# Attention, mixer and FFN on one core: transposed scores, row sums as a value column, the mixer inside the attention loop, a token-major FFN with a table gelu

## The chip, the cores and the metric

The kernel runs on one core of one Trainium2 chip. The metric is the device time of one execution in microseconds; the kernel before took 1292.27 us, the median of three runs. A NeuronCore has five engines with an instruction queue each: TensorE (PE, matmuls into PSUM), VectorE (DVE), ScalarE (ACT), GpSimd (POOL) and SyncE (SP), which here issues transfers. They run side by side and wait for one another through semaphores; within a queue the order is fixed when the program is built.

## What is computed

```python
xn = layernorm(A_x)                                    # [2048, 576]
# attention: 32 query heads, 16 key/value heads, the last 512 keys of the cache
q = (xn @ wq).reshape(1, 2048, 32, 128).transpose(0, 2, 1, 3)
k = repeat(k_cache[:, :, 1536:, :], 2, axis=1); v = the same of v_cache
scores = einsum("bhqd,bhkd->bhqk", q, k) * 128 ** -0.5
s = softmax(scores) @ v, heads joined, @ wo            # [2048, 576]
# branch B, from the same xn
h  = gelu_tanh(layernorm(xn) @ w1)                     # four groups of 144 columns
hs = concat(h[g] shifted by +1, -1, +2, -2 tokens) @ w2
x1 = xn + hs
h2 = gelu_tanh(layernorm(x1) @ w3) @ w4                # w3 [576, 4608]
out = A_x + s * silu(x1 + h2)
```

All inputs are bf16, with normal entries times 0.05 (weights also divided by the root of their rows).

## The kernel before

Tokens go in four blocks of 512 (`QB`), each of four tiles of 128 rows; the model width 576 is four chunks of 128 and one of 64, so a projection is five accumulating matmuls of 512 columns. Program order is written by hand in Python loops; each engine takes its instructions in that order as far as its queue is concerned, and pools of SBUF and PSUM buffers add the waits.

Part A (0 to 782 us of the trace) runs over blocks and, within one, over 32 heads; one head of one block is called a unit below. `stage1(h)` makes the projection (L257), copies it to SBUF on ACT (`qT_hb`, L261), and for each tile of 128 tokens makes scores `[token, key]` (L270), the negated row maximum on DVE (L272), the exponential on ACT with that maximum as bias and the row sum as accumulator (L274), and on DVE the reciprocal (L279) and the scaling of the probabilities (L281). `stage2(h)`, two heads later, turns the probabilities round: for each of four key chunks four 128x128 transposes on TensorE (L292), a copy to SBUF (three on DVE, L298, one on ACT, L296), and one product with the values (L299, 512 columns), and then a copy of the head's output on ACT (L301). The output projection `wo` of the block before (L339, 512 and 64 columns for each head and token tile) is cut into pieces of eight heads, one piece a step; that of the last block stands alone at the end. The four normalized blocks go to DRAM (`xn_dram`) and the output projection's result to `s_dram`.

Part B loads xn again, loads and rearranges w1, w2 and w3, and runs the mixer block by block (782 to 899 us): a second layernorm with a square root on ACT (L115), transposes (L440), the up product with a five-step gelu on DVE and ACT (L446 to L456), the shifted down product of eight chunks a tile (four big, four with 16 rows; L487, L494), the addition (L500), a third layernorm and its transposes (L510, L512). Then the FFN (899 to 1287 us): for each block 36 steps of an up product with 4608/36 = 128 outputs (L580), the gelu chain copy (L556), square (L558), polynomial (L560), product (L563), Sigmoid on ACT (L565), product (L566), and two steps later a down product with weights w4 as the stationary side (L590), so that the result comes out with features on partitions; it is copied (L594), turned back by transposes (L599), and joined on DVE and ACT with x1, silu, s and A_x (L602 to L618).

Of the kernel before, what the change touches and what calls it, by code (L numbers as in the profile page):

```python
# [27 lines left out]
def kernel(  # L28
# [14 lines left out]
    nc = tc.nc  # L43

    Bb, S, D = A_x.shape
    assert Bb == 1
    _, Hkv, Sk, Dh = A_k_cache.shape
    assert Dh == P
    HqDh = A_wq.shape[1]
    Hq = HqDh // Dh  # L50
# [3 lines left out]
    assert W % P == 0  # L54
    KCH = W // P
    F = B_w3.shape[1]
    assert F % P == 0
# [3 lines left out]
    assert S % QB == 0  # L61
# [3 lines left out]

    DCH = []
    st = 0
    while st < D:
        w = min(P, D - st)
        DCH.append((st, w))  # L70
        st += w
    NDC = len(DCH)
    DLAST_W = DCH[-1][1]
    OSPLIT = []
    st = 0
    while st < D:
        w = min(512, D - st)
        OSPLIT.append((st, w))
        st += w
# [9 lines left out]
    const_pool = ctx.enter_context(tc.tile_pool(name="const_pool", bufs=1))  # L89
    ident = const_pool.tile([P, P], BF16, name="ident")  # L90
    make_identity(nc, ident)

    xn_dram_pool = ctx.enter_context(tc.tile_pool(name="xn_dram_pool", bufs=1, space=bass.MemoryType.DRAM))
    xn_dram = xn_dram_pool.tile([S, D], BF16, name="xn_dram")
    s_dram_pool = ctx.enter_context(tc.tile_pool(name="s_dram_pool", bufs=1, space=bass.MemoryType.DRAM))
    s_dram = s_dram_pool.tile([S, D], BF16, name="s_dram")

    eps_t = const_pool.tile([P, 1], FP32, name="eps_t")
    nc.vector.memset(eps_t[:], LN_EPS)

    def layernorm_rows(dsts, srcs, pool):
        n = len(srcs)
        ngrp = 1
        while D // ngrp > nc.vector.BN_STATS_FMAX or D % ngrp != 0:
            ngrp += 1
        fsz = D // ngrp
        mv = pool.tile([P, n, nc.vector.BN_AGGR_DIM], FP32, name="ln_mv")
        for i, src_ap in enumerate(srcs):
            stats = pool.tile([P, ngrp, nc.vector.BN_STATS_DIM], FP32, name="ln_stats")
            srcr = src_ap.rearrange("p (n f) -> p n f", f=fsz)  # L110
            for j in range(ngrp):
                nc.vector.bn_stats(out=stats[:, j, :], in_=srcr[:, j, :])
            nc.vector.bn_aggr(out=mv[:, i, :], in_=stats[:])
        rstd = pool.tile([P, n], FP32, name="ln_rstd")
        nc.scalar.activation(out=rstd[:, :], in_=mv[:, :, 1], func=ACT.Sqrt, bias=eps_t[:], scale=1.0)  # L115
        nc.vector.reciprocal(out=rstd[:, :], in_=rstd[:, :])
        for i, (dst_ap, src_ap) in enumerate(zip(dsts, srcs)):
            nc.vector.tensor_scalar(out=dst_ap, in0=src_ap, scalar1=mv[:, i, 0:1], scalar2=rstd[:, i:i + 1],
                                    op0=ALU.subtract, op1=ALU.mult)

    def _unused_transpose_tokens_to_T(src_tm, dstT, ps_pool, name):
        for b in range(NB):
            for kc, (cst, cw) in enumerate(DCH):
                ps = ps_pool.tile([P, QB], BF16, name=name, tag="tp")
                for tt in range(TB):
                    t = b * TB + tt
                    nc.tensor.transpose(out=ps[:cw, tt * P:(tt + 1) * P], in_=src_tm[:, t, cst:cst + cw],
                                        identity=ident[:, :])
                nc.scalar.activation(out=dstT[:cw, kc, b * QB:(b + 1) * QB], in_=ps[:cw, :], func=ACT.Copy)

    with ExitStack() as actx:
        a_big = actx.enter_context(tc.tile_pool(name="a_big", bufs=1))
        xnT = a_big.tile([P, NDC, S], BF16, name="xnT")
        if DLAST_W < P:
            nc.vector.memset(xnT[DLAST_W:, NDC - 1, :], 0.0)
        kT = a_big.tile([P, Hkv, W], BF16, name="kT")
        v_sb = a_big.tile([P, Hkv, KCH, Dh], BF16, name="v_sb")
        wo_sb = a_big.tile([P, Hq, D], BF16, name="wo_sb")
        oT_blks = [a_big.tile([P, Hq, QB], BF16, name=f"oT_blk{i}") for i in range(min(NB, 2))]
        xraw = actx.enter_context(tc.tile_pool(name="xraw", bufs=min(NB, 3)))  # L140
        xload = actx.enter_context(tc.tile_pool(name="xload", bufs=1))
        pro_small = actx.enter_context(tc.tile_pool(name="pro_small", bufs=4))
        wo_out = actx.enter_context(tc.tile_pool(name="wo_out", bufs=2))
        a_ld = actx.enter_context(tc.tile_pool(name="a_ld", bufs=2))
        wq_pool = actx.enter_context(tc.tile_pool(name="wq_pool", bufs=2))
        qt_pool = actx.enter_context(tc.tile_pool(name="qt_pool", bufs=3))
        p_pool = actx.enter_context(tc.tile_pool(name="p_pool", bufs=3))
        pt_pool = actx.enter_context(tc.tile_pool(name="pt_pool", bufs=4))
        small = actx.enter_context(tc.tile_pool(name="a_small", bufs=8))
        ps_tp = actx.enter_context(tc.tile_pool(name="ps_tp", bufs=2, space=bass.MemoryType.PSUM))  # L150
        ps_q = actx.enter_context(tc.tile_pool(name="ps_q", bufs=1, space=bass.MemoryType.PSUM))
        ps_sc = actx.enter_context(tc.tile_pool(name="ps_sc", bufs=4, space=bass.MemoryType.PSUM))
        ps_o = actx.enter_context(tc.tile_pool(name="ps_o", bufs=1, space=bass.MemoryType.PSUM))
# [495 lines left out]
```

## Time and profile before

| | us |
|---|---|
| median of three runs | 1292.27 (1289.19 to 1296.06) |
| span of the profiled execution | 1287.0 |
| attention, to the last output product | 0 to 782 |
| mixer, with the reload ahead of it | 782 to 899 |
| FFN | 899 to 1287 |
| busy over the span: TensorE, VectorE, ScalarE | 1073.4, 988.5, 829.3 |

The rows used are listed below. Busy time is the sum of what each record covers. Records of TensorE's matmuls overlap with those of their neighbours (a 512-column matmul is shown with about 380 ns), so what an engine can do in a stretch is read from the distance between starts. A row of the timeline joins several instructions of one line: its time is from the first start to the last end. "Idle before" is time in which the engine waited ahead of that group, with what ended the wait.

### The profile page before, as it was taken

To read this page: it belongs to the slowest core of one execution; us is meant where nothing else is said; L and a number is where in the kernel's file an instruction comes from. 1 tells how busy PE (TensorE), PEld (TensorE's weight loads), DVE (VectorE), ACT (ScalarE), POOL (GpSimd) and SP (SyncE) were. 2 spreads that over 40 slices of the span, in tenths; PEclk is the share of its full clock that TensorE was granted. 3 is DMA by queue.
4 is the path that set the end of the run, shared out by engine and by line. 5 is a ranking of instruction groups with operands and counts; after the bars stand their busy time and mean duration, and the time that the engine had idled before them with its cause. 6 is when DMAs were issued, how large, how long until landed. Compare 5 with 4: busy or idle time off the path is not lost.

```text
span 1287.0 us, 19414 instructions
## 1 busy us (share of the span) xinstructions
PE 1073.4 (83%) x6788; PEld 534.2 (42%) x6916; DVE 988.5 (77%) x2703; ACT 829.3 (64%) x1876; POOL 27.8 (2%) x41
## 2 busy tenths in 40 slices
PE   4777788998879997789997893696998898998995
PEld 2344444554445554445444451343433333433432
DVE  7999988788997879988889932796666766666665
ACT  5787887778887778877778830564545444544544
POOL 4100000000000000000000001001000000000000
PEclk9999999999999999999999997799999999998998
DMA  9402101001010010101101006213300101001001
GB/s 301 124 28 69 50 24 38 29 25 42 20 37 24 24 43 24 38 19 35 36 24 38 1 10 230 76 38 102 106 1 15 41 1 32 25 1 40 16 1 37
DMA packets 49954, 59.94 MB, mean 47 GB/s; under 512 B 11712, under 2 KB 46208, under 8 KB 49280
## 3 DMA queue, kind: packets, MB, share of 16 engines
q1 hardware_dynamic: 41968, 35.87, 9.2%
q0 software_dynamic: 3760, 13.97, 3.5%
q10 hardware_dynamic: 4128, 8.85, 2.1%
q8 instruction: 54, 0.88, 0.3%
q14 instruction: 44, 0.36, 0.1%
HBM read 51.60 MB, written 7.08 MB: 46 GB/s over the span
## 4 chain that ended last, share of the span: by engine, by line
PE 32%; ACT 30%; DVE 25%; issue 9%; DMA 3%; ACTq 0%; POOL 0%; SPq 0%; DVEq 0%
ACT p_blk L274 16%; PE pswo L339 7%; PE pso L299 6%; PE sc L270 5%; ACT g_hb L556 5%; DVE g_sq L558 4%; DVE g_arg L563 4%; DVE negmax L272 4%; DVE pT L298 3%; PE ptp L292 3%; DVE p_blk L281 3%; DVE g_u L560 3%; PE psq L257 3%; ACT oT_blk L301 2%; PE ps_h L590 2%
## 5 line engine op out<-in xcount | busy, mean ns | idle before, releaser
L274 ACT ACTIVATE p_blk<-sc,negmax 128x512 bf16<-128x512 f32 x512 | 346.6, 688 | 86.3 <-DVE negmax L272 85.0
L272 DVE TENSOR_REDUCE negmax<-sc 128x1 f32<-128x512 f32 x512 | 324.9, 684 | 28.6 <-PE sc L270 26.6
L299 PE MATMUL pso<-pT,v_sb 128*128 128x512 bf16 x512 | 187.4, 380 | 81.4 <-DVE pT L298 69.3
L565 ACT ACTIVATE g_sg<-g_arg 128x512 bf16<-128x512 bf16 x144 | 90.8, 631 | 179.7 <-DVE g_arg L563 179.5
L590 PE MATMUL ps_h<-h3g,w_sb 128*128 128x512 bf16 x718 | 177.3, 378 | 28.8 <-DVE h3g L566 15.4
L292 PEld LDWEIGHTS <-p_blk 128*128 128x128 bf16 x2048 | 145.5, 98 | 128.6 <-issue 59.2
L292 PE MATMUL ptp<-ident,p_blk 128*128 128x128 bf16 x2048 | 178.6, 219 | 7.3 <-DVE pT L298 3.0
L580 PE MATMUL ph<-x1nT,w_sb 128*128 128x512 bf16 x692 | 179.3, 386 | 4.6 <-ACT g_hb L556 2.2
L270 PE MATMUL sc<-kT,qT_hb 128*128 128x512 bf16 x496 | 154.6, 381 | 18.4 <-ACT qT_hb L261 16.0
L298 DVE COPY pT<-ptp 128x512 bf16<-128x512 bf16 x384 | 154.6, 413 | 17.7 <-PE ptp L292 16.5
L257 PE MATMUL psq<-xnT,wq_slab 128*128 128x512 bf16 x606 | 163.0, 381 | 2.1 <-ACT qT_hb L261 0.6
L339 PE MATMUL pswo<-wo_sb,oT_blk 128*128 128x512 bf16 (+1 forms) x985 | 157.6, 282 | 2.1 <-ACT p_blk L274 0.7
L281 DVE TENSOR_SCALAR p_blk<-p_blk,rinv 128x512 bf16<-128x512 bf16 x512 | 156.4, 348 | 2.0
L566 DVE TENSOR_TENSOR h3g<-g_hb,g_sg 128x512 bf16<-128x512 bf16 x144 | 61.3, 426 | 97.4 <-ACT g_sg L565 96.7
L590 PEld LDWEIGHTS <-w_sb 128*128 128x128 bf16 x720 | 69.6, 97 | 133.1 <-issue 61.6
L580 PEld LDWEIGHTS <-w_sb 128*128 128x128 bf16 x720 | 71.2, 99 | 90.7 <-issue 9.2
L274 ACT ACTIVATION_READ_ACCUMULATOR p_blk<-sc,negmax 128x1 f32 x512 | 105.0, 205 | 0.0
L339 PEld LDWEIGHTS <-oT_blk 128*128 128x128 bf16 x1024 | 73.8, 98 | 67.3 <-issue 11.3
L301 ACT ACTIVATE oT_blk<-pso 128x512 bf16<-128x512 f32 x128 | 76.3, 596 | 35.7 <-PE pso L299 35.7
L296 ACT ACTIVATE pT<-ptp 128x512 bf16<-128x512 bf16 x128 | 76.9, 601 | 23.9 <-PE ptp L292 23.9
L299 PEld LDWEIGHTS <-v_sb 128*128 128x128 bf16 x512 | 49.8, 98 | 95.6 <-DVE pT L298 57.1
L556 ACT ACTIVATE g_hb<-ph 128x512 bf16<-128x512 f32 x144 | 83.6, 581 | 7.5 <-PE ph L580 4.6
(84 smaller groups left out, 857.4 us busy)
## 6 DMA issues: line engine op xcount, KB each, us to landing
wq_slab<-in_A_wq_dram SPq DMA_DIRECT2D x30, 512.0 KB, 3.5
w_sb<-in_B_w_dram POOLq DMA_DIRECT2D x4, 1296.0 KB, 12.2
wo_sb<-in_A_wo_dram POOLq DMA_DIRECT2D x4, 1152.0 KB, 13.5
w_sb<-in_B_w_dram ACTq DMA_DIRECT2D x1, 4608.0 KB, 18.5
xn_dram<-xnb SPq DMA_DIRECT2D x4, 576.0 KB, 3.2
s_dram<-s_out SPq DMA_DIRECT2D x16, 144.0 KB, 1.8
xnb<-xn_dram SPq DMA_DIRECT2D x4, 576.0 KB, 4.7
xnt<-xn_dram ACTq DMA_DIRECT2D x16, 144.0 KB, 2.1
```

What stands on the lines that cost most here:

```text
L257: nc.tensor.matmul(psq[:, :], lhsT=wq_slab[:, kc, hh * Dh:(hh + 1) * Dh], rhs=xnT[:, kc, qb * QB:(qb + 1) * QB], start=(kc == 0), stop=(kc ...
L270: nc.tensor.matmul(sc[:, :W], lhsT=qT_hb[:, qc * P:(qc + 1) * P], rhs=kT[:, g, :], start=True, stop=True)
L272: nc.vector.tensor_reduce(out=negmax[:, qc:qc + 1], in_=sc[:, :W], axis=AX.X, op=ALU.max, negate=True)
L274: nc.scalar.activation(out=p_blk[:, qc, :], in_=sc[:, :W], func=ACT.Exp, bias=negmax[:, qc:qc + 1], scale=1.0, accum_out=rowsum[:, qc:qc + 1])
L281: nc.vector.tensor_scalar_mul(out=p_blk[:, qq, :], in0=p_blk[:, qq, :], scalar1=rinv[:, qq:qq + 1])
L292: nc.tensor.transpose(out=ptp[:, qc * P:(qc + 1) * P], in_=p_blk[:, qc, kc * P:(kc + 1) * P], identity=ident[:, :])
L298: nc.vector.tensor_copy(out=pT[:, :], in_=ptp[:, :])
L299: nc.tensor.matmul(pso[:, :], lhsT=v_sb[:, g, kc, :], rhs=pT[:, :], start=(kc == 0), stop=(kc == KCH - 1))
L339: nc.tensor.matmul(ps[:, :dw], lhsT=lhsT, rhs=wo_sb[:, h, dst:dst + dw], start=(h == 0), stop=(h == Hq - 1))
L556: nc.scalar.activation(out=hb[:, :], in_=ps_ap, func=ACT.Copy)
L580: nc.tensor.matmul(ph3[:, :], lhsT=w3_sb[:, kc, fc * P:(fc + 1) * P], rhs=x1nT[:, kc, b * QB:(b + 1) * QB], start=(kc == 0), stop=(kc == N ...
L590: nc.tensor.matmul(ph2s[dc][:, :], lhsT=w4_sb[:, fc2, dc * P:(dc + 1) * P], rhs=h3g[:, :], start=(fc2 == 0), stop=(fc2 == FC - 1))
```

## The change

Attention is one loop over 128 units with four stages. `stage_q(u+1)` is the projection and its copy. `stage_s(u)` makes the scores transposed: key chunk as the stationary side, `sc` is `[128 keys, 512 tokens]`, and one exponential with the score scale gives `pT`, with no maximum and no bias. `stage_v(u-1)` takes slices of `pT` as weights and the values with an added column of ones (`VW = Dh + 2`, 129 columns used) as the moving side, so that column 129 of the result is the row sum; DVE takes its reciprocal and multiplies. `stage_t(u-2)` transposes the head's output, with a DVE copy. A table `fill` puts the other work at fixed units: the output projection of the block before at units 2 to 6 of a block, the second layernorm, its transposes and the mixer's up product at 8 to 15, its down product at 16 to 20 (of the block before; of the last block also at 22 to 26), the next block's layernorm and transposes at 21 to 26. xn stays in SBUF, x1 goes to `x1_dram`. The layernorm takes its square root by three Newton steps on DVE.

That no maximum is subtracted is covered by a bound: DVE finds the largest absolute weight of wq (eight slabs, in the first block) and of the keys, and `flag_i` is set where their product times `BOUND` (6581.9) passes 40. At the end every engine reads the flag, and where it is set, attention runs once more tile by tile with the maximum subtracted and the result is written anew.

The FFN makes its up product as before with one `Gelu_apprx_tanh` out of PSUM on ACT; the down product takes the gelu's slices as weights and w4 as the moving side (512 and 64 columns for each token tile), so that no transposes follow; silu is written with Tanh. The last block makes all 36 up products first and then the down products tile by tile. PSUM in attention: three score banks, one for projections and the mixer's up product, one for transposes, two for products, one for the output projection and the mixer's down product.

```diff
-                psq = ps_q.tile([P, QB], FP32, name="psq")
...
-                    nc.tensor.matmul(sc[:, :W], lhsT=qT_hb[:, qc * P:(qc + 1) * P], rhs=kT[:, g, :],
-                                     start=True, stop=True)
-                    nc.vector.tensor_reduce(out=negmax[:, qc:qc + 1], in_=sc[:, :W], axis=AX.X,
-                                            op=ALU.max, negate=True)
-                    nc.scalar.activation(out=p_blk[:, qc, :], in_=sc[:, :W], func=ACT.Exp,
-                                         bias=negmax[:, qc:qc + 1], scale=1.0,
-                                         accum_out=rowsum[:, qc:qc + 1])
...
+            for kc in range(KCH):
+                sc = ps_sc.tile([P, QB], FP32, name="sc", tag="sc")
+                nc.tensor.matmul(sc[:, :], lhsT=kT[:, g, kc * P:(kc + 1) * P], rhs=qT[:, :], start=True, stop=True)
+                pT = pT_pool.tile([P, QB], BF16, name="pT")
+                nc.scalar.activation(out=pT[:, :], in_=sc[:, :], func=ACT.Exp, scale=SCALE)
+                pTs.append(pT)
...
+            for t0 in range(0, TB, 2):
+                po = ps_po.tile([P, 2, Dh + 1], FP32, name="po", tag="po")
+                for j in range(2):
+                    tt = t0 + j
+                    for kc in range(KCH):
+                        nc.tensor.matmul(po[:, j, :], lhsT=pTs[kc][:, tt * P:(tt + 1) * P],
+                                         rhs=v_sb[:, g, kc, 0:Dh + 1], start=(kc == 0), stop=(kc == KCH - 1))
+                ri = small.tile([P, 2], FP32, name="ri")
+                nc.vector.reciprocal(out=ri[:], in_=po[:, :, Dh])
+                nc.vector.tensor_tensor(out=o[:, t0:t0 + 2, :], in0=po[:, :, 0:Dh],
+                                        in1=ri[:].unsqueeze(2).to_broadcast([P, 2, Dh]), op=ALU.mult)
...
+        def b1(b, c):
...
+            ph = ps_pq.tile([P, QB], FP32, name="ph", tag="pq")
...
+            x = g1_pool.tile([P, QB], BF16, name="g_x")
+            nc.vector.tensor_copy(out=x[:], in_=ph[:, :])
...
+        for b in range(NB):
+            base = b * Hq
+            if b > 0:
+                for i, unit in enumerate(wo_units(b - 1)):
+                    at(base + 2 + i // 4, unit)
+            at(base + 8, lambda b=b: ln2(b))
...
+        for j in range(8):
+            at(4 * j + 1, lambda j=j: nc.vector.tensor_reduce(
+                out=mx[:, j:j + 1], in_=wq_b[j % NWQ][:].rearrange("p a b -> p (a b)"), axis=AX.X, op=ALU.max,
+                apply_absolute_value=True))
...
+            h3 = hp.tile([P, QB], BF16, name="h3")
+            nc.scalar.activation(out=h3[:, :], in_=ph[:, :], func=ACT.Gelu_apprx_tanh)
...
+            nc.tensor.matmul(pm[tt][:, :], lhsT=lhsT, rhs=w4[:, fc % WS, 0:M0], start=(fc == 0), stop=(fc == FC - 1))
+            nc.tensor.matmul(pr[:, tt, :], lhsT=lhsT, rhs=w4[:, fc % WS, M0:D],
+                             start=(fc == 0 and tt == 0), stop=(fc == FC - 1), skip_group_check=True)
```

TensorE around the last score of a unit, steady attention, before (`ptp`: turned probabilities, `pso`: product with the values, `pswo`: output pass):

```order
L339 MATMUL pswo_3411<-wo_sb,oT_blk_79 128x512
L270 LDWEIGHTS qT_hb
L270 MATMUL sc<-kT,qT_hb 128x512
L339 LDWEIGHTS oT_blk_79
L339 MATMUL pswo_3412<-wo_sb,oT_blk_79 128x64
L299 LDWEIGHTS v_sb
L299 MATMUL pso<-pT,v_sb 128x512
```

The same engine and place after; ahead of these rows stand five projection matmuls, three scores and six more products of the unit before, behind them six more products:

```order
L285 LDWEIGHTS pT
L285 MATMUL po<-v_sb,pT 128x129
L270 LDWEIGHTS kT
L270 MATMUL sc<-qT,kT 128x512
L285 LDWEIGHTS pT
L285 MATMUL po<-v_sb,pT 128x129
```

The loads of weights are now keys and probabilities, and the products that stand round the fourth score belong to the unit before; the output pass is no longer scattered between them.

VectorE in steady attention, before (two units' stages are mixed):

```order
L272 TENSOR_REDUCE negmax<-sc 128x1 x4
L279 RECIPROCAL rinv<-rowsum 128x2
L298 COPY pT<-ptp 128x512
L281 TENSOR_SCALAR p_blk<-p_blk,rinv 128x512 x2
L279 RECIPROCAL rinv<-rowsum 128x2
L298 COPY pT<-ptp 128x512
L281 TENSOR_SCALAR p_blk<-p_blk,rinv 128x512 x2
L298 COPY pT<-ptp 128x512
```

VectorE after, one unit:

```order
L288 RECIPROCAL ri<-po 128x2
L289 TENSOR_TENSOR o<-po,ri 128x256
L288 RECIPROCAL ri<-po 128x2
L289 TENSOR_TENSOR o<-po,ri 128x256
L299 COPY oT<-ps_o 128x512
```

Of 12 operations of the unit before, maxima, scalings and three copies are gone; five operations are left.

SyncE's transfers at the end of attention, before (`w_sb`, `w_big`, `w_sel`: weights of the mixer):

```order
L348 DMA s_dram<-s_out 128x576 x3
L411 DMA w_sb<-in_B_w_dram 128x4x576
L348 DMA s_dram<-s_out 128x576
L413 DMA w_sb<-in_B_w_dram 64x576
L415 DMA w_big<-in_B_w_dram 128x576 x3
L378 DMA xnb<-xn_dram 128x4x576
```

SyncE after (`x_dram` is `x1_dram`, `s_b` and `x_b` are for the FFN's end; L519 to L522 load the FFN's first slab of w3 and w4):

```order
L551 DMA s_b<-s_dram 128x4x576
L553 DMA x_b<-in_A_x_dram 128x4x576
L512 DMA x_9929<-x_dram 128x4x576
L330 DMA s_dram<-s_out 128x4x576
L519 DMA w_s_9882<-in_B_w_dram 128x4x512
L521 DMA w_s_9882<-in_B_w_dram 64x512
L522 DMA w_s_9891<-in_B_w_dram 128x4x576
```

The mixer's weights and the reload of xn have left this place, and the FFN's weights, in nine slabs, stand behind the store of the last output pass.

## Rows read from the trace of the kernel before

**Rows 1.** The page: its head, and TensorE's busy tenths in 40 slices.

```profile
span 1287.0 us, 19414 instructions
...
PE   4777788998879997789997893696998898998995
```

**Rows 2.** Stretches: length, busy PE, PEld, DVE, ACT, POOL; granted clock, DMA share, GB/s.

```profile
18.00:782.00 764.00, 651.93 (x4758) 347.23 (x4845) 647.22 (x1770) 584.70 (x1447) 8.82 (x12) 1.00 0.13 40
180.00:700.00 520.00, 459.03 (x3336) 242.44 (x3397) 447.13 (x1212) 403.56 (x1010) 0.00 (x0) 1.00 0.09 29
782.00:812.00 30.00, 1.37 (x9) 0.64 (x9) 14.59 (x50) 3.00 (x6) 5.25 (x8) 0.56 0.86 283
782.00:899.00 117.00, 74.80 (x508) 38.05 (x517) 84.17 (x266) 55.16 (x96) 9.36 (x12) 0.82 0.37 116
899.00:1287.00 388.00, 340.43 (x1490) 145.51 (x1519) 248.12 (x640) 184.22 (x326) 0.00 (x0) 0.98 0.09 28
```

**Rows 3.** Groups by line: busy us, mean ns of one, idle before and releasers.

```profile
L274 ACT ACTIVATE p_blk<-sc,negmax 128x512 bf16<-128x512 f32 x512 | 346.6, 688 | 86.3 <-DVE negmax L272 85.0
L272 DVE TENSOR_REDUCE negmax<-sc 128x1 f32<-128x512 f32 x512 | 324.9, 684 | 28.6 <-PE sc L270 26.6 <-PE pso L299 0.2
...
L292 PE MATMUL ptp<-ident,p_blk 128*128 128x128 bf16 x2048 | 178.6, 219 | 7.3 <-DVE pT L298 3.0 <-DVE p_blk L281 2.8 <-DVE kT L186 0.6
...
L298 DVE COPY pT<-ptp 128x512 bf16<-128x512 bf16 x384 | 154.6, 413 | 17.7 <-PE ptp L292 16.5
...
L292 PEld LDWEIGHTS <-p_blk 128*128 128x128 bf16 x2048 | 145.5, 98 | 128.6 <-issue 59.2 <-DVE p_blk L281 3.2
...
L565 ACT ACTIVATE g_sg<-g_arg 128x512 bf16<-128x512 bf16 x144 | 90.8, 631 | 179.7 <-DVE g_arg L563 179.5
...
L301 ACT ACTIVATE oT_blk<-pso 128x512 bf16<-128x512 f32 x128 | 76.3, 596 | 35.7 <-PE pso L299 35.7
...
L279 DVE RECIPROCAL rinv<-rowsum 128x2 f32<-128x2 f32 x256 | 41.3, 161 | 35.4 <-ACT p_blk L274 25.8
```

**Rows 4.** Timeline at five places: start, length, engine, line, operation, count, idle before.

```profile
17.81 1.04 PE L270 MATMUL sc<-kT,qT_hb 128*128 128x512 bf16 x4 [0.26 <-ACT qT_hb L261]
...
204.71 0.61 PE L292 MATMUL ptp<-ident,p_blk 128*128 128x128 bf16 x8
...
989.26 2.52 ACT L594 ACTIVATE h2T<-ps_h 128x512 bf16<-128x512 f32 x5 [0.92 <-PE ps_h L590]
...
1002.30 2.32 PE L590 MATMUL ps_h<-h3g,w_sb 128*128 128x512 bf16 x10 [2.79 <-DVE h3g L566]
...
1283.31 0.46 DVE L617 TENSOR_TENSOR fo<-fsg,fxt 128x576 bf16<-128x576 bf16 x1 [0.92 <-DMA fxt<-in_A_x_dram]
1283.80 0.34 SPq L618 DMA_DIRECT2D out_dram<-fo  x1
```

**Rows 5.** TensorE's groups by shape from 229.48 to 229.57 us.

```profile
L339 PE MATMUL pswo<-wo_sb,oT_blk 128*128 128x512 bf16 x1 | 0.4, 377 | 0.0
L339 PE MATMUL pswo<-wo_sb,oT_blk 128*128 128x64 bf16 x3 | 0.2, 190 | 0.0
```

**Rows 6.** TensorE's groups by shape from 758 to 780 us.

```profile
L339 PE MATMUL pswo<-wo_sb,oT_blk 128*128 128x512 bf16 x89 | 22.3, 380 | 0.0
L339 PE MATMUL pswo<-wo_sb,oT_blk 128*128 128x64 bf16 x91 | 17.5, 193 | 0.2
```

**Rows 7.** The additions out of PSUM (L500) by shape, whole span.

```profile
L500 DVE TENSOR_TENSOR x<-psx,xnt 128x512 bf16<-128x512 f32 x16 | 11.0, 687 | 4.2 <-PE psx L494 4.1
L500 DVE TENSOR_TENSOR x<-psx,xnt 128x64 bf16<-128x64 f32 x16 | 3.5, 216 | 0.0
```

**Rows 8.** The page's DMA issues: one slab of wq; size, us from issue to landing.

```profile
wq_slab<-in_A_wq_dram SPq DMA_DIRECT2D x30, 512.0 KB, 3.5
```

More of the change, by code (lines that the diff above doesn't have):

```diff
@@ L60 @@
     QB = 512
-    assert S % QB == 0
     NB = S // QB
@@ L64 @@
     SCALE = float(Dh) ** -0.5
[L66 to L79, printed above, removed]
+    NF = D // P
+    DR = D - NF * P
+    NDC = NF + 1
+    DCH = [(i * P, min(P, D - i * P)) for i in range(NDC)]
+    M0 = 512
+    R0 = D - M0
     c4 = D // 4
-    assert c4 > P and c4 - P <= 32, "layout assumes D//4 = 128 + r with r <= 32"
     rsz = c4 - P
@@ L121, in _unused_transpose_tokens_to_T @@
[L121 to L129, printed above, removed]
@@ new lines, with stage_q @@
+        qT_t, pT_t, o_t, oT_t = {}, {}, {}, {}
+        def stage_q(u):
+            qb, h = divmod(u, Hq)
+            w = wq_b[(u // 4) % NWQ]
+            hh = h % 4
+            psq = ps_pq.tile([P, QB], FP32, name="psq", tag="pq")
+            for kc in range(NDC):
+                nc.tensor.matmul(psq[:, :], lhsT=w[:, kc, hh * Dh:(hh + 1) * Dh], rhs=xnT_b[qb % 2][:, kc, :],
+                                 start=(kc == 0), stop=(kc == NDC - 1))
+            qT = qT_pool.tile([P, QB], BF16, name="qT")
+            nc.scalar.activation(out=qT[:, :], in_=psq[:, :], func=ACT.Copy)
+            qT_t[u] = qT
@@ new lines, in b2, with b2_rem @@
+        def b2(b, tt):
+            ps = ps_wo.tile([P, M0], FP32, name="psx1", tag="wo")
+            b2_mm(ps[:, :], b, tt, 0, M0)
+            nc.vector.tensor_tensor(out=x1_t[b][:, tt, 0:M0], in0=ps[:, :], in1=xn_t[b][:, tt, 0:M0], op=ALU.add)
+        def b2_rem(b):
+            ps = ps_wo.tile([P, TB, R0], FP32, name="psx1r", tag="wo")
+            for tt in range(TB):
+                b2_mm(ps[:, tt, :], b, tt, M0, D)
+            nc.vector.tensor_tensor(out=x1_t[b][:, :, M0:D], in0=ps[:, :, :], in1=xn_t[b][:, :, M0:D], op=ALU.add)
+            nc.sync.dma_start(out=rows(x1_dram, b * TB, TB), in_=x1_t.pop(b)[:])
+            xn_t.pop(b)
@@ new lines @@
+        at(36, finish_flag)
+        prep_kT(0)
+        ln1(0)
+        for kc in range(NDC):
+            tr1(0, kc)
+        stage_q(0)
+        last = max(fill)
+        for u in range(0, max(U + 2, last) + 1):
+            if u + 1 < U:
+                stage_q(u + 1)
+            if u < U:
+                stage_s(u)
+            if 0 <= u - 1 < U:
+                stage_v(u - 1)
+            if 0 <= u - 2 < U:
+                stage_t(u - 2)
+            for fn in fill.get(u, []):
+                fn()
```

966 lines of the change are left out of this document (492 added, 474 removed).

## The prediction

> **What bounds the kernel now.** I read the page's 40 slices first: TensorE is near full in every slice but the two around 800 us [rows 1]. So there are three stretches: attention to 782, a hole with the mixer behind it to 899, the FFN. The table by stretch [rows 2] gives each its limit. In steady attention (180 to 700) TensorE is busy 459.03 of 520 us, VectorE (DVE) 447.13, ScalarE (ACT) 403.56: three engines nearly full, passing data round a ring. The costliest groups say with what [rows 3]: per head and block four maxima on DVE at 684 ns, four exponentials on ACT at 688, four scalings, and 16 transposes with their copies, to turn the probabilities round. From 782 to 899 TensorE is busy 74.80 of 117 us, and 1.37 of the first 30. In the FFN it is busy 340.43 of 388; ScalarE waits there 179.7 us for DVE's polynomial [rows 2, 3], off TensorE's path.
>
> Busy time is not work, since records of successive matmuls overlap; work is the distance of their starts. Ten 512-column matmuls cover 2.32 us with 0.38 for the last one [rows 6]: 216 ns apart. Eight transposes (128 columns) cover 0.61 with a last one of 0.219: 56 apart [rows 3, 4]. Three 64-column matmuls of 0.19 start within 0.09 us: about 28 apart [rows 5]. All load fresh weights. Some 90 pairs of 512 and 64 columns fill 22 us, 244 a pair, the sum of the two [rows 6]. Five PSUM copies on ACT cover 2.52 us at 0.6 each: 0.48 apart [rows 3, 4].
>
> **Attention.** Per head and block TensorE now has 5 projections, 4 scores, 4 products and 16 transposes: 13 x 216 + 16 x 56 = 3704 ns, beside the output pass. Afterwards the scores come out with keys on partitions, and the probabilities are at once the weights of the next product: 9 x 216, 16 products of 129 columns (56.2 by the same step per column) and 4 transposes, 1944 + 899 + 224 = 3067 ns. The rest of the gain is that the ring opens. DVE keeps two reciprocals (161 [rows 3]), two 128x256 multiplications out of PSUM and a copy of 413. Additions out of PSUM take 687 at 512 columns and 216 at 64 [rows 7]: 1.05 ns a column, so 418 at 256. Together 0.32 + 0.84 + 0.41 = 1.57 us a unit. ACT has five operations 0.48 apart, 2.4 us. Neither is the bound.
>
> The exponential without a per-row bias and accumulator is not in the trace. Its nearest rows are the PSUM copy, 596, and the present one, 688 [rows 3]; I take the copy, which like it has one tile as its only input. One unit then goes: projections end at 1.08, three scores at 1.73. The projection's copy holds ACT from 1.28, so the first exponential runs from 1.76 to 2.36. After eight products TensorE stands at 2.18 before the fourth score, which needs one of three score banks: it starts at 2.41, one wait of 0.23, and nothing else is late. A unit takes 3.29 us; with 688 the wait is 0.32, 12 us in all. 128 x 3.29 = 421, behind a first score at 18 as now [rows 4], since the loads and the normalization that lead there stay.
>
> **Woven in, on the same TensorE:** the output pass 512 x (216 + 28) = 125; mixer up 20 groups x 5 x 216 = 22; mixer down, five chunks instead of eight, 16 x 5 x 244 = 19; some 200 transposes, 11: 177. Their waits: a mixer-up group shares the one projection bank, which DVE's copy now frees (413 [rows 3]): 0.45 x 20 = 9. The eight maxima of the weights run over 128x2560 in one piece, 2560 x 1.05 = 2.7 us on DVE's queue ahead of the multiplications; DVE has 1.7 of 3.3 us free, so about 1 of each comes through, 8. Together 17, at least 0 and at most 20 x 0.9 + 8 x 2.7 = 40. The square root goes from ACT to some fourteen tiny DVE operations (161 each by the reciprocal's row, 2.3 us), beside TensorE's work.
>
> **The seam.** The mixer's stretch of 117 us [rows 2] goes; 41 of it came back above. Next late is the FFN's first weight slab, whose buffer lies on attention's and whose load stands on SP's queue behind the last output matmul. SP's transfers ahead of it are issued during the last output pass. Evacuation 0.6, issue 0.4, 3.5 for half a megabyte [rows 8], and a cool start (granted clock 0.56 in 782 to 812 [rows 2], between 1.2 and 2.4 GHz) for the first groups, 4.5: 9 us. The single output bank adds 0.7 at each of the last four tiles: 3. Bounds for the 12: 3, if the slab hides, and 31, if the hole of 28 before the mixer stays.
>
> **FFN.** Up 720 x 216 = 155.5, down 576 x 244 = 140.5 (token-major, with a 64-column remainder), transposes 3.5: 299.5; now it is 2 x 155.5 and the turning back, when ACT alone copies for 2.52 us a block [rows 4]. The one gelu, at 0.6 to 0.69, stands beside 2.06 us of matmuls a chunk, and beside 1.08 in the last block, where all up groups come first: nothing; without cover it would be 0.6 x 144 = 86, but three up banks keep it. At three block ends DVE must read four result banks before the next down matmuls: 2 x (0.69 + 0.22), the gate's two, two and two operations (0.75 for the f32 one by 1.05 a column, 0.46 [rows 4]) and two more reads, 7 us, against four up groups, 4.3: 2.5 each, 7.5 (0 to 12). The tail: sum 0.9, tanh 0.7 (631 at 512 columns [rows 3]), three DVE operations 1.7, issue to end of span 3.2 [rows 4], and a flag read and branch for which there is no row, 0 to 4: 9 (6 to 13).
>
> **Sum.** 18 + 421 + 177 + 17 + 12 + 299.5 + 7.5 + 9 = 961. The profiled execution has a span of 1287.0 [rows 1] against the runs' median of 1292.27, so 5.3 is added: **966 us**. All waits at their lower ends take off 28, 17, 9, 7.5 and 3: 902. The upper ends add 12, 23, 19, 4.5 and 4: 1029.
>
> **Rivals.**
> (a) The unit is paced by hand-offs, as now: the projections and the turning back each have one bank, and TensorE's queue is strict. Today's work of 3.70 and 125/128 for the output pass is 4.68 us a unit, against 764/128 = 5.97 that it takes [rows 2], 78%. At 78% the new unit takes 3.07/0.78 = 3.91 us, 128 x 0.62 = 79 more: **1045**. For it: the projection's copy stands in ACT's queue among the exponentials. Against: it is asked for a unit ahead, and the ring of DVE and ACT operations that fills the other 22% is gone.
> (b) Narrow matmuls paced by their weight loads: a load's record is 98 ns [rows 3], and the runs seen at 56 and 28 are no longer than ten and three [rows 4, 5], while the new products stand 16 in a row and the remainder pass 128. If loads no longer overlap, 2048 x 42 + 592 x 70 = 127 us: **1093**. Against: transposes in eights pay nothing at their end. The Trainium skill, "TensorE: Matmul & The Clock Gate" (Back-to-back issue gap), has a rule of this kind: in a sustained stream of weight load and matmul, 128 columns are some 81 ns apart and not 56. By it, as an estimate, the sum would be 966 + 2048 x 25 + 592 x 53 ns = 1048. The trace agrees with its isolated gap and not with its stream, at up to ten in a row; longer runs it doesn't show.
> (c) Slower than before: TensorE waits for its own unit's exponentials. Copy 0.6, four exponentials 2.04, a hand-off of 0.26 [rows 4] would lie bare in each unit: 3.07 + 2.9 = 5.97, 343 us more, **1309**; from 5.84 a unit on, the kernel is no faster. Against: by the order of TensorE the products of the unit before stand behind a unit's scores, so the exponentials have a whole unit's time.
> (d) It doesn't do what it says: the flag is set and attention runs a second time, in its slow form with no overlap of heads. Even at the pace of 764 us now [rows 2] that is 966 + 764 = **1730**. The inputs give 0.00604 (largest weight) x 0.1445 (largest key) x 6582 = 5.75 against a limit of 40.
> (e) Nearly no waits: **902**.
>
> **How the numbers follow.** Forecast 0.78, (a) 0.12, (b) 0.04, (c) 0.02, (d) 0.01, (e) 0.03. The likeliest gives 966. The range runs from 925, below which over half of the waits must vanish, to 1050, which takes in the upper ends and (a); (b), (c), (d) and (e) stay outside, with some of the forecast's own spread. About 0.5% is what a measurement of this kernel can tell from no change; within it 0.01, slower 0.02, faster 0.97.
>
> **What would show it.** A unit (from one first projection to the next, where no work is woven in) should take 3.2 to 3.4 us: at 3.9 with products 56 apart it is (a), with products 80 or more apart it is (b), with over 1 us of waiting ahead of the first product (c). The exponential should last 0.6 to 0.69, with a wait of 0.2 ahead of the fourth score. From the last output matmul to the first FFN matmul: 9 us, clock low behind it. The FFN should take 315 to 320. If units and FFN are right and the total isn't, the woven work or the seam was mis-sized.

## The result and the profile after

The changed kernel took 988.35 us, the median of four runs (987.75 to 988.83), against 1291.71 us before; the ratio is 0.7649, with a 95% interval of 0.7632 to 0.7665. The forecast was 966 us, 925 to 1050. The time lies in the range, 22 us above the forecast. The profiled execution spans 986.0 us where the sum said 961, so 25 us are to be explained.

The page after, its head and TensorE's tenths in 40 slices, answers to [rows 1]:

```profile
span 986.0 us, 17237 instructions
...
PE   0799979999999999999999999979599999999996
```

The hole before the mixer is gone; what is left is a short one at the seam and, new, a whole slice and more at the start in which TensorE does almost nothing.

The stretches after, with columns as in [rows 2]: up to the first score, attention, the last output pass, the seam, the FFN, the tail, and once more the first 3 us of the FFN alone.

```profile
0.00:37.40 37.40, 8.01 (x39) 3.93 (x39) 22.71 (x65) 1.88 (x2) 15.98 (x31) 1.00 1.05 272
37.40:617.00 579.60, 565.51 (x4888) 342.67 (x4887) 324.27 (x1053) 346.84 (x672) 15.76 (x26) 0.99 0.15 45
617.00:654.40 37.40, 34.63 (x300) 18.64 (x298) 9.57 (x39) 3.70 (x8) 0.11 (x1) 1.00 0.25 80
654.40:661.20 6.80, 2.07 (x21) 1.17 (x20) 3.13 (x8) 1.53 (x2) 5.58 (x11) 0.96 0.83 253
661.20:977.00 315.80, 304.89 (x1932) 147.42 (x1931) 62.34 (x181) 94.88 (x159) 8.11 (x15) 0.98 0.19 58
977.00:986.00 9.00, 0.00 (x0) 0.00 (x0) 2.44 (x5) 0.68 (x1) 0.54 (x1) 0.75 0.12 39
...
661.20:664.20 3.00, 3.00 (x8) 1.03 (x8) 0.00 (x0) 0.60 (x1) 0.00 (x0) 0.52 1.09 329
```

Laid beside the sum, stretch by stretch:

| stretch | forecast, us | measured, us |
|---|---|---|
| to the first score | 18 | 37.4 |
| attention with woven work and last output pass | 421 + 177 + 17 + 3 = 618 | 617.0 |
| seam (4.5 of the 9 were for a low clock behind it) | 9 | 6.8, and 1.4 at the low clock, which lie in the next row |
| FFN | 299.5 + 7.5 = 307 | 315.8 |
| tail | 9 | 9.0 |

TensorE is now the bound nearly everywhere: in attention it is busy 565.51 of 579.6 us, VectorE 324.27 and ScalarE 346.84. Two stretches carry the error, the start (+19.4) and the FFN (+8.8), and the attention that agrees to 1 us does so because of errors of both signs, as the experiments show.

One plain unit of the timeline after shows the mechanism that the forecast walked through:

```profile
301.36 0.81 PE L270 MATMUL sc<-qT,kT 128*128 128x512 bf16 x3
301.56 0.60 ACT L261 ACTIVATE qT<-psq 128x512 bf16<-128x512 f32 x1 [1.00 <-PE psq L258]
302.01 0.63 PE L285 MATMUL po<-v_sb,pT 128*128 128x129 bf16 x8
302.06 2.06 ACT L272 ACTIVATE pT<-sc 128x512 bf16<-128x512 f32 x4
302.68 0.17 DVE L288 RECIPROCAL ri<-po 128x2 f32<-128x2 f32 x1 [1.44 <-PE po L285]
302.70 0.38 PE L270 MATMUL sc<-qT,kT 128*128 128x512 bf16 x1
302.88 0.42 DVE L289 TENSOR_TENSOR o<-po,ri 128x256 bf16<-128x256 f32 x1
302.92 0.63 PE L285 MATMUL po<-v_sb,pT 128*128 128x129 bf16 x8
303.38 0.38 PE L297 MATMUL ps_o<-ident,o 128*128 128x128 bf16 x4
303.60 1.24 PE L258 MATMUL psq<-xnT_b,wq_b 128*128 128x512 bf16 x5
```

Eight products start at 302.01 and are 0.059 us apart, so the eighth makes room for the next matmul at 302.48; the fourth score starts only at 302.70, when the first exponential of the group that began at 302.06 (0.6 us) has freed its bank. That is the one wait of 0.22 us. A unit's projection copies on ScalarE start 3.32 us apart (forecast 3.29).

The groups by line, with the terms that were priced from neighbours:

```profile
L272 ACT ACTIVATE pT<-sc 128x512 bf16<-128x512 f32 x512 | 265.4, 610 | 30.0 <-PE sc L270 29.9
L285 PE MATMUL po<-v_sb,pT 128*128 128x129 bf16 x2048 | 163.1, 220 | 0.2 <-DVE o L289 0.2
L289 DVE TENSOR_TENSOR o<-po,ri 128x256 bf16<-128x256 f32 x256 | 107.2, 420 | 5.0
...
L461 DVE TENSOR_REDUCE mx<-wq_b 128x1 f32<-128x2560 bf16 x8 | 22.6, 2819 | 10.1 <-DMA wq_b<-in_A_wq_dram 10.1
L359 DVE CAST g_x<-ph 128x512 bf16<-128x512 f32 x20 | 13.8, 689 | 3.2 <-PE ph L356 2.7
```

The exponential is 610 ns (taken: 596), the multiplication out of PSUM 420 (418), a maximum of a slab 2.82 us (2.7).

### The profile page after: what moved, and what is told of

Its sections match the earlier page's. It is cut to its first block, busy times and chain, and to the rows that moved or that the text cites. A ratio compares the mean times of both kernels' runs of the same rounds, so it can differ in the third digit from the quotient of the medians.

```text
span 986.0 us, 17237 instructions
## 1 busy us (share of the span) xinstructions
PE 915.1 (93%) x7172; PEld 513.8 (52%) x7172; DVE 424.5 (43%) x1349; ACT 449.5 (46%) x842; POOL 46.1 (5%) x84
## 4 chain that ended last, share of the span: by engine, by line
PE 74%; ACT 10%; DVE 5%; DMA 5%; SPq 3%; issue 2%; POOL 0%; ACTq 0%; DVEq 0%; POOLq 0%
PE ph L563 15%; PE psq L258 13%; PE pm L572 12%; PE pswo L315 11%; PE po L285 7%; PE sc L270 6%; ACT qT L261 5%; ACT pT L272 4%; PE ps_o L297 3%; PE ph L356 2%; DMA wq_b<-in_A_wq_dram 2%; PE pr L573 2%; DMA k_nat<-in_A_k_cache_dram 2%; PE psx L392 2%; PE pswr L326 1%
## 5 line engine op out<-in xcount | busy, mean ns | idle before, releaser
L272 ACT ACTIVATE pT<-sc 128x512 bf16<-128x512 f32 x512 | 265.4, 610 | 30.0 <-PE sc L270 29.9
L563 PE MATMUL ph<-x1nT,w_s 128*128 128x512 bf16 x720 | 176.2, 385 | 3.8 <-DMA w_s<-in_B_w_dram 3.8
L285 PEld LDWEIGHTS <-pT 128*128 128x128 bf16 x2048 | 140.1, 98 | 67.1 <-issue 17.6
L258 PE MATMUL psq<-xnT_b,wq_b 128*128 128x512 bf16 x640 | 164.0, 381 | 0.9 <-DVE g_x L359 0.5
L285 PE MATMUL po<-v_sb,pT 128*128 128x129 bf16 x2048 | 163.1, 220 | 0.2 <-DVE o L289 0.2
L270 PE MATMUL sc<-qT,kT 128*128 128x512 bf16 x512 | 155.2, 380 | 6.5
L572 PE MATMUL pm<-w_s,h 128*128 128x512 bf16 x576 | 154.6, 380 | 0.1
L315 PE MATMUL pswo<-wo_sb,oT 128*128 128x512 bf16 x512 | 115.2, 379 | 2.1 <-ACT s_out L318 2.1
L573 PE MATMUL pr<-w_s,h 128*128 128x64 bf16 x576 | 108.1, 193 | 0.0
L572 PEld LDWEIGHTS <-h 128*128 128x128 bf16 x576 | 56.1, 98 | 66.2
L573 PEld LDWEIGHTS <-h 128*128 128x128 bf16 x576 | 55.4, 98 | 11.1
```

The lines of the kernel that those rows point to most:

```text
L258: nc.tensor.matmul(psq[:, :], lhsT=w[:, kc, hh * Dh:(hh + 1) * Dh], rhs=xnT_b[qb % 2][:, kc, :], start=(kc == 0), stop=(kc == NDC - 1))
L270: nc.tensor.matmul(sc[:, :], lhsT=kT[:, g, kc * P:(kc + 1) * P], rhs=qT[:, :], start=True, stop=True)
L272: nc.scalar.activation(out=pT[:, :], in_=sc[:, :], func=ACT.Exp, scale=SCALE)
L285: nc.tensor.matmul(po[:, j, :], lhsT=pTs[kc][:, tt * P:(tt + 1) * P], rhs=v_sb[:, g, kc, 0:Dh + 1], start=(kc == 0), stop=(kc == KCH - 1))
L315: nc.tensor.matmul(st["ps"][:, :], lhsT=oT_t[qb * Hq + h][:, tt * P:(tt + 1) * P], rhs=wo_sb[:, h, 0:M0], start=(h == 0), stop=(h == Hq - 1))
L563: nc.tensor.matmul(ph[:, :], lhsT=w3[:, kc, f0:f0 + P], rhs=x1nT[b % 2][:, kc, :], start=(kc == 0), stop=(kc == NDC - 1))
```

## Where the first 37 us go

TensorE waits for the normalized input (`xn`), as the first of these rows shows, and VectorE's rows show a queue that stands still:

```profile
28.70 1.31 PE L233 MATMUL ps_t<-ident,xn 128*128 128x128 bf16 x4 [19.61 <-DVE xn L118]
...
7.17 0.17 DVE L95 TENSOR_SCALAR nr_y<-nr_v 128x4 int32<-128x4 int32 x1
8.17 2.82 DVE L461 TENSOR_REDUCE mx<-wq_b 128x1 f32<-128x2560 bf16 x1 [0.82 <-DMA wq_b<-in_A_wq_dram]
...
13.48 0.17 DVE L101 TENSOR_SCALAR nr_t<-nr_t 128x4 f32<-128x4 f32 x1
21.04 2.82 DVE L461 TENSOR_REDUCE mx<-wq_b 128x1 f32<-128x2560 bf16 x1 [7.39 <-DMA wq_b<-in_A_wq_dram]
23.78 0.15 DVE L103 TENSOR_TENSOR nr_y<-nr_y,nr_t 128x4 f32<-128x4 f32 x1
25.91 0.69 DVE L242 TENSOR_REDUCE mx<-k_nat 128x1 f32<-128x512 bf16 x1 [1.97 <-DMA k_nat<-in_A_k_cache_dram]
...
28.21 1.45 DVE L118 TENSOR_SCALAR xn<-xt,ln_mv,nr_y 128x576 bf16<-128x576 bf16 x4
```

The first normalization is a chain of short operations (`nr_t`, `nr_y`). In the built order the maxima for the bound stand between them: of the second slab of wq, which lands at 21 us, and of key groups that land at 26 and 27. The normalization needs neither, but VectorE takes its instructions in order. It ends at 29.7 us, where in the kernel before it ended at 11.8:

```profile
10.39 1.45 DVE L118 TENSOR_SCALAR xnb<-xt,ln_mv,ln_rstd 128x576 bf16<-128x576 bf16 x4
```

The rival is that the loads alone hold the start, as the DMA share is 1.05 in this stretch.

**All maxima away** (the bound is not checked in this run):

```diff
-            nc.vector.tensor_reduce(out=mx[:, 8 + g:9 + g], in_=k_nat[:].rearrange("p a b -> p (a b)"), axis=AX.X,
-                                    op=ALU.max, apply_absolute_value=True)
...
-        at(36, finish_flag)
...
+    nc.vector.memset(flag_i[:], 0)
```

> Left out: all maxima of weights and keys and the flag's arithmetic (the flag is set to zero), so the bound is not checked. In the changed kernel the first score starts at 37.4 us; ahead of it VectorE waits for the second slab of wq (to 21 us) and the third key group (to 27 us), both for maxima that stand in its queue inside the first normalization. Theory (strict queue): without them the first score starts at 18 to 21 us, the 5.4 us hole at 142 us goes together with the slower clock behind it (3.4 us), and some 1 us for each of eight maxima: 988 becomes 953 to 963. Rival (the loads of the first 37 us, at 272 GB/s, hold the first units whatever VectorE does): the first score stays past 28 us or the first units wait for keys, values and weights, and the time is 972 or more.

964.88 us (963.87 to 965.85). The first score of that run, in its timeline:

```profile
20.59 1.49 PE L269 MATMUL sc<-qT,kT 128*128 128x512 bf16 x3
```

20.6 instead of 37.4 us: the theory of the queue holds for the start, and the loads, at the same bandwidth (276 GB/s over the first 37.4 us), don't hold the first score. They hold TensorE a little later: at 44.5 us it waits 2.19 us for a slab of wq. The total missed the expected band by 2 us: the 1 us for each of eight maxima that I had in it is not there. From the first score to the first projection of the second block the changed kernel takes 125.5 us, 3.65 of them for output-pass work that had slipped in from the second block; without maxima it takes 115.1. The 6.8 between is about what the flag's hole costs (7.0, below). The hole in the FFN, another matter, was 12.22 us in this run instead of 10.97.

**All maxima kept, in another place:** those of the weights in the second block's units, on the slabs loaded again there, those of the keys on the transposed keys:

```diff
-            at(4 * j + 1, lambda j=j: nc.vector.tensor_reduce(
+            at(Hq + 4 * j + 1, lambda j=j: nc.vector.tensor_reduce(
...
+        for g in range(Hkv):
+            at(2 * Hq + g + 8, lambda g=g: nc.vector.tensor_reduce(
+                out=mx[:, 8 + g:9 + g], in_=kT[:, g, :], axis=AX.X, op=ALU.max, apply_absolute_value=True))
-        at(36, finish_flag)
+        at(2 * Hq + 26, finish_flag)
```

> All maxima stay, in another place: those of the weights in the second block's units, on the slabs that are loaded again there, those of the keys on the transposed keys, behind their copies; the flag's arithmetic follows in the third block, still inside attention. Theory (the place in VectorE's queue costs, not the work): the first score starts at 18 to 21 us as without any maxima (20.5 us), the hole for the flag's read back stays (5 us and the slower clock behind it), now in the third block: 988 becomes 968 to 974. Rival (the maxima's work of 22.6 and 10.8 us costs wherever it stands): 980 or more.

970.84 us (969.66 to 971.33), in the expected band, and the first score at 19.6 us:

```profile
19.62 0.81 PE L268 MATMUL sc<-qT,kT 128*128 128x512 bf16 x3
```

Nothing was taken out and 17.5 us are gone. It was the place, not the work. That 17.5 is close to the 17.8 by which the first score came earlier is partly chance, for two other things changed. TensorE now waits for a slab of wq at 44.7 us and works at a granted clock of 0.54 from 45.0 to 50.5 us, nearly all of it at the lower level of 1.2 GHz. And the read-back of the flag, expected to keep its 5 us and to stand in the third block, came in the second and holds TensorE only briefly (the second of these rows):

```profile
44.70 2.31 PE L256 MATMUL psq<-xnT_b,wq_b 128*128 128x512 bf16 x5 [3.60 <-DMA wq_b<-in_A_wq_dram]
...
290.11 0.64 PE L283 MATMUL po<-v_sb,pT 128*128 128x129 bf16 x8 [1.71 <-DVE o L287]
```

## The hole for the flag

Near the end of the first block TensorE stands for 5.4 us between a projection and the transposes of the next block's input. VectorE and TensorE there:

```profile
146.44 0.41 DVE L415 TENSOR_REDUCE mm<-m 1x2 f32<-1x256 f32 x1 [5.33 <-DMA m<-mx_dram]
```

```profile
141.86 0.81 PE L258 MATMUL psq<-xnT_b,wq_b 128*128 128x512 bf16 x3
147.70 0.59 PE L233 MATMUL ps_t<-ident,xn 128*64 128x128 bf16 x4 [5.03 <-DVE oT L299]
```

The maxima go to DRAM and come back as one row; the reduction of that row waits 5.33 us in VectorE's queue, with a unit's multiplications and copies behind it. The stretches of this hole and of the one in the FFN, and of the matmuls that follow each, show the price of the clock (columns as above):

```profile
142.40:147.80 5.40, 0.37 (x4) 0.21 (x3) 1.36 (x6) 0.00 (x0) 0.00 (x0) 0.76 0.28 80
147.80:152.10 4.30, 4.30 (x23) 2.47 (x23) 1.08 (x4) 2.31 (x5) 0.00 (x0) 0.50 0.00 0
689.40:700.40 11.00, 0.23 (x4) 0.13 (x2) 6.34 (x28) 0.00 (x0) 0.00 (x0) 0.74 0.24 76
700.40:705.10 4.70, 4.70 (x18) 2.06 (x17) 1.66 (x5) 0.60 (x1) 0.00 (x0) 0.51 0.00 0
```

Behind each hole TensorE works 4.3 and 4.7 us at a granted clock of 0.50 and 0.51, which is 1.2 of 2.4 GHz, and so loses another 2.2 and 2.3 us.

```diff
-            m1 = small.tile([1, 2, P], FP32, name="m1", bufs=1)
-            nc.gpsimd.dma_start(out=m1[:], in_=mx_dram[:, :].rearrange("(o p) c -> o c p", o=1))
...
+        def flag_tail():
+            w = fin.tile([P, D], FP32, name="bs")
+            m1 = w[0:1, 0:2 * P].rearrange("o (c p) -> o c p", c=2)
+            nc.gpsimd.dma_start(out=m1, in_=mx_dram[:, :].rearrange("(o p) c -> o c p", o=1))
...
+                    if b == 1 and step == 20:
+                        flag_tail()
```

> Only the second half of the flag's arithmetic (the maxima read back from DRAM as one row, their maximum and product) is moved from attention into the FFN, behind the first block's end. Theory: the 5.4 us hole at 142 us is VectorE waiting in its queue for that read, and 6.8 us at the lower clock behind it cost another 3.4: 988 becomes 978 to 982. Rival (the next block's input or transposes are late by themselves): the hole stays, 986 to 989.

981.36 us (979.66 to 984.56), 7.0 less, in the band. From 135 to 155 us TensorE was busy 14.91 of 20 us at a clock of 0.83 in the changed kernel and is now:

```profile
135.00:155.00 20.00, 19.57 (x182) 12.75 (x183) 11.01 (x37) 14.20 (x29) 0.55 (x1) 1.00 0.12 35
```

## The hole in the FFN

At 689.4 us TensorE comes to the transposes of the second block's normalized x1 and waits. SyncE, VectorE and TensorE, in three places of the timeline:

```profile
683.79 0.59 SPq L522 DMA_DIRECT2D w_s<-in_B_w_dram  x1
684.42 0.95 SPq L512 DMA_DIRECT2D x<-x_dram  x1
...
693.50 1.18 DVE L114 BATCH_NORM_STATS2 ln_st<-x 128x6 f32<-128x288 bf16 x3 [35.65 <-DMA x<-x_dram]
...
700.25 0.29 PE L535 MATMUL ps_x<-ident,xm 128*128 128x128 bf16 x1 [10.77 <-DVE xm L118]
```

The load of x1 (L512) is issued behind the last of nine weight slabs, at 684.4 us, lands at 693.5, and 6.7 us of normalization follow.

```diff
         load_w(0)
+        load_x1(1)
         ln3(0)
...
-            if not lastb:
+            if not lastb and b > 0:
                 load_x1(b + 1)
```

> Only the load of x1 for the FFN's second block is issued behind the first weight slab instead of behind all nine. Theory: the hole of 10.97 us at 689 us, where TensorE waits for that block's transposes, is the wait for this load on SP's queue; it goes, with about 3 us of matmuls at the lower clock behind it: 988 becomes 973 to 977. Rival (the slabs themselves are as late, so that the up products wait in its place): 984 to 988.

975.10 us (973.78 to 977.03), 13.3 less, in the band. The FFN of that run:

```profile
661.20:964.40 303.20, 300.51 (x1893) 146.70 (x1932) 62.28 (x180) 94.88 (x159) 8.14 (x16) 0.99 0.20 62
```

303.2 instead of 315.8 us, with TensorE busy all but 2.7 of them.

## The wait of each unit, and the terms priced from neighbours

**The fourth score behind all sixteen products:**

```diff
-                stage_s(u)
+                stage_s(u, 0, 3)
             if 0 <= u - 1 < U:
                 stage_v(u - 1)
+            if u < U:
+                stage_s(u, 3, 4)
```

> Only the place of each unit's fourth score changes: behind all sixteen products of the unit before instead of behind eight. Theory: the 0.22 us wait ahead of it is for one of three score banks, and nobody needs this score's exponential before the next unit's products; a unit falls from 3.32 to 3.10 us, 28 us over 128 units, 958 to 963. Rival (the fourth exponential, now later, holds the next unit's products, or ScalarE's queue holds the next projection's copy): the wait moves, 980 to 990.

971.29 us (969.22 to 974.16): 17 less, between the two expectations. The timeline shows the wait gone:

```profile
311.85 1.10 PE L284 MATMUL po<-v_sb,pT 128*128 128x129 bf16 x16
312.79 0.38 PE L270 MATMUL sc<-qT,kT 128*128 128x512 bf16 x1
```

A plain unit fell from 3.32 to 3.10 us, as expected. My expectation was too large by its count. Taken from the distances of starts, the wait between products and a score occurs some 105 times in the changed kernel and adds up to 23 us; the rest of the units hide it under woven work. In this run it is 0.3 us. The profiled execution, the slowest of the four, spans 972.4 us, 13.6 less than that of the changed kernel. In it the second to fourth block got 5 us shorter each and the first 0.8 longer, because TensorE waits there for VectorE twice more (2.57 and 1.83 us), behind maxima of wq whose slabs come late for the faster units, as in this row:

```profile
50.21 2.82 DVE L460 TENSOR_REDUCE mx<-wq_b 128x1 f32<-128x2560 bf16 x1 [2.57 <-DMA wq_b<-in_A_wq_dram]
```

**A bias of zeros for the exponential:**

```diff
-                nc.scalar.activation(out=pT[:, :], in_=sc[:, :], func=ACT.Exp, scale=SCALE)
+                nc.scalar.activation(out=pT[:, :], in_=sc[:, :], func=ACT.Exp, bias=zero_b[:], scale=SCALE)
```

> The exponentials get a per-row bias of zeros from SBUF, as the kernel before had the negated maximum; nothing else changes. Theory (the term as priced): an exponential takes 688 instead of 600 ns, the wait ahead of the fourth score rises from 0.22 to 0.31 us in about 100 units: 996 to 1001. Rival (the bias costs nothing beside the accumulator that the kernel before had with it): 986 to 990.

993.02 us (990.5 to 995.21; ratio 0.7694, 0.7669 to 0.7719), 4.7 more and so between the two. The operation got as long as expected:

```profile
L274 ACT ACTIVATE pT<-sc,zero_b 128x512 bf16<-128x512 f32 x512 | 310.9, 694 | 28.4 <-PE sc L272 26.9 <-PE ps_o L299 1.3
```

694 against 610 ns, so the bias alone makes up the 688 of [rows 3], and the accumulator that stood beside it before had no part in them that shows. The fourth score came 0.09 us later, as worked out, but in the built order it now stands behind nine products and not eight, which covers 0.06 of that: the unit is 3.35 us. The Trainium skill's "ScalarE: Activation LUTs" (What ACT_TABLE_LOAD costs) gives about 93 ns for a per-partition operand; the difference of 84 here comes near it.

**Every gelu twice:**

```diff
             h3 = hp.tile([P, QB], BF16, name="h3")
+            nc.scalar.activation(out=h3[:, :], in_=ph[:, :], func=ACT.Gelu_apprx_tanh)
             nc.scalar.activation(out=h3[:, :], in_=ph[:, :], func=ACT.Gelu_apprx_tanh)
```

> Every gelu of the FFN is computed twice, the second into the same tile: 144 more operations of 0.6 us on ScalarE, 86 us busy. Theory (gelu is covered, and was rightly costed at nothing): 0.96 us of ScalarE against steps of 2.06 us and, in the last block, of 1.08 us; 988 to 991. Rival (the last block's steps are at their limit, and up banks come free later): 995 or more.

990.11 us (988.66 to 990.88; ratio 0.7662, 0.7640 to 0.7684), not told apart from the changed kernel. Costing the gelu at nothing was right, in the last block too.

**The polynomial chain in place of the table, the rest as it is:**

```diff
-            nc.scalar.activation(out=h3[:, :], in_=ph[:, :], func=ACT.Gelu_apprx_tanh)
+            nc.scalar.activation(out=x[:], in_=ph[:, :], func=ACT.Copy)
+            nc.vector.tensor_tensor(out=u[:], in0=x[:], in1=x[:], op=ALU.mult)
+            nc.vector.tensor_scalar(out=u[:], in0=u[:], scalar1=GELU_B, scalar2=GELU_A, op0=ALU.mult, op1=ALU.add)
...
+            nc.scalar.activation(out=th[:], in_=u[:], func=ACT.Tanh)
...
+            nc.vector.tensor_tensor(out=h3[:, :], in0=x[:], in1=th[:], op=ALU.mult)
```

> The FFN keeps its token-major form, but the one gelu becomes the chain again (copy on ScalarE, square, polynomial, product on VectorE, tanh on ScalarE, two more operations on VectorE), in the form that the mixer has here. VectorE then has about 1.9 us a chunk against TensorE's step of 2.06 us, and against 1.08 us in the last block's 36 up groups. Theory (the table gelu matters only where it is uncovered, in the last block): 36 x 0.8 = 29 us more, and some at the three block ends: 1015 to 1035. Rival (the chain's latency is late in every step, as in the kernel before, whose FFN lasted 388 us): 1050 or more. Rival (even the last block is covered by the three up banks): 988 to 995.

1028.88 us (1026.33 to 1032.89), 40 more, in the expected band but not for the reason given. The last block lost 11 us, not 29, and the second and third some 12 to 13 each, much of it behind the block ends, in rows such as these of TensorE:

```profile
756.30 6.42 PE L564 MATMUL ph<-x1nT,w_s 128*128 128x512 bf16 x28
...
767.49 0.61 PE L582 MATMUL pm<-w_s,h 128*128 128x512 bf16 x1 [4.77 <-DVE h L576]
```

VectorE has to read the result banks, run the gate and feed the chain there, and TensorE waits 4.77 us for the chain's last operation, and 4.26 at each of the other two ends. Its waits for that operation add up to 25.8 us over the FFN, so the three ends are about half of them; the rest are shorter waits within the blocks. So, with the rest as it is, the table gelu is worth 40 us, about a third of which these three ends show.

**The four moves together:**

> All four moves together: maxima late, the flag's second half in the FFN, x1 of the second block ahead of the slabs, the fourth score behind all products. Theory (four separate waits): 988 less 17 (first score), 8 (flag), 13 (x1) and 17 (fourth score, as measured alone) is 933, 928 to 938. Rival (waits of attention hide in one another, or the loads of the first 40 us then hold the faster units): 945 or more.

937.62 us (936.00 to 939.11), ratio 0.7255 (0.7232 to 0.7278): in the band, 50.7 us below the changed kernel, and so below both. The four moves alone gave 17.5, 7.0, 13.3 and 17.1, together some 55: the waits are nearly separate, and 4 us are lost in the sum. One part of that was counted twice, since the moved maxima by themselves had already cut the wait behind the flag's read to 1.71 us; no run takes the 4 us apart further.

**And the last output pass on the score banks:**

```diff
-                            st["ps"] = ps_wo.tile([P, M0], FP32, name="pswo", tag="wo")
+                            if qb == NB - 1:
+                                st["ps"] = ps_sc.tile([P, M0], FP32, name="pswo", tag="sc")
+                            else:
+                                st["ps"] = ps_wo.tile([P, M0], FP32, name="pswo", tag="wo")
```

> As the run with all four moves (937.6 us), and in the last block the output pass takes the score banks, which are free by then, in place of the one output bank. Theory: the four waits of 1.06 us between token tiles at 590 to 615 us fall to 0.22, 3.4 us less: 933 to 936. Rival (the evacuations are then late for the FFN's first banks): 937 or more.

935.08 us (933.72 to 936.85), ratio 0.7251 (0.7241 to 0.7261), in the band, though the interval doesn't separate it from the run before. Its trace shows the four waits gone, where the other still has rows such as the second of these (first this run, then the one before):

```profile
583.82 26.71 PE L315 MATMUL pswo<-wo_sb,oT 128*128 128x512 bf16 x121
```

```profile
591.83 7.07 PE L312 MATMUL pswo<-wo_sb,oT 128*128 128x512 bf16 x32 [0.69 <-ACT s_out L315]
```

## Why the prediction was right, and where it was off

- **The unit: right.** 3.32 us against 3.29, with the wait at the fourth score that had been walked out (0.22, forecast 0.23). The 0.03 is the 129-column product: 58 to 59 ns between starts, not 56.2, sixteen times, less the 0.01 of the wait. That the ring of hand-offs cost the kernel before its other 22% is argued from its rows; the runs here put back only the bias (4.7 us) and the gelu chain (40 us).
- **Rival (b) falls, and with it the skill's rule.** Sixteen products with fresh weights stand 0.059 us apart and the 64-column matmuls of the remainder pass 0.029, in runs of 128. The 81 ns of the Trainium skill, "TensorE: Matmul & The Clock Gate" (Back-to-back issue gap), for a sustained stream of 128-column matmuls do not appear here. Rivals (a) and (c) fall with the unit's 3.32 us, (d) did not occur, and (e), 902, falls with the time.
- **The start: the step that failed.** The prediction said "behind a first score at 18 as now, since the loads and the normalization that lead there stay". They stay, but maxima for the bound were ordered into the normalization, with their waits for DMA: +19.4 us. The sum charges the maxima of the weights to the units of the first block and has none for the keys; the order of the built program showed both in the normalization. Moving them brought the first score from 37.4 to 19.6 us, so some 1.6 of the 19.4 are not theirs. The first paragraph also calls TensorE near full in every slice but two; the first slice, with 4 tenths in [rows 1], is not, and it is the stretch with the largest error.
- **The FFN: a term missing, one too large.** The forecast names SP's queue at the seam, but only for the first slab; the load behind all nine slabs was left out: 11 us and 2.3 at the low clock, measured together as 13.3. The three block ends were put at 2.5 us each and took about 0.2, since TensorE's order mixes the next up groups with the first down matmuls. The prediction's last part asked for 315 to 320 us; the 315.8 fit by chance, as the terms made 307, or 316 with the tail, against 324.8.
- **The woven work: right in sum, wrong in parts.** From the distances of starts TensorE loses 3.5 us ahead of the mixer-up groups, mostly for the projection's copy on ScalarE, which holds the shared bank, and 1.6 behind them for `g_x`: 5.1, forecast 9, although the copy `g_x` is 689 ns and not 413. The maxima's work, as work, cost nothing that can be seen, forecast 8; their waits for DMA did. The wait at the fourth score, forecast in all 128 units (29 us), came to 23. Against these stand the flag's round trip through DRAM, 7.0 us, which I had not priced, and 4 us of slower products (128 x 0.03). That 617.0 meets 618 so closely is luck.
- **The seam: right in sum, both parts off. The tail: right.** At the seam the first weight slab was waited for 6.8 us where 4.5 were forecast, as it lands 5.9 us after its first issue at 655.1 (forecast 3.5), with eight more slabs behind it; the low clock cost 1.4 (3.0 us at a granted clock of 0.52) where 4.5 were forecast. The tail is 9.0 against 9. The last four evacuations made steps of 1.06 us, 0.84 more than a matmul's, where 0.7 was forecast.
- **From span to time.** I added 5.3 us to the span, from the run before; after it is 2.4, which hides 3 us of the miss.

## What to carry to other kernels

A new side job, here the bound that allows a shorter main path, costs less by its work than by the place that it gets in a queue: look in the built order for each instruction that waits for a DMA, and ask what stands behind it, in the first microseconds above all. Loads that are issued late in one long list (the second block's input behind nine weight slabs) belong in front of what is not needed sooner. Where an engine becomes the bound, the work that it does per unit, taken from the distance of starts, gave its time to 1%; nearly all of the error was in waits for DMA, at the start and in the FFN. And a wait that is taken away lets the next one show: the faster starts brought out waits for a slab of wq.

## What the runs showed of the hardware

Loads of the first 37 us run at 272 GB/s, with the DMA share at 1.05; a key group issued at 8.16 us has landed only by 25.9, eighteen us later, while a slab of wq lands in 3.7 us at the median of all, by the page of the profile. After the holes of 5.4 and 11 us TensorE worked for 4.3 and 4.7 us at half the clock (granted 0.50 and 0.51), which makes 40 and 21% more than the length of the holes; without them the kernel was 7.0 and 13.3 us faster, 30 and 21% more than their length.
